# Twenty-four weight pieces narrowed in two groups instead of three, and a block's additions written ahead of its low parts

## The chip, the core and the metric

The kernel runs on one core of a Trainium2 chip. The core has five engines that work side by side, each through its own instructions in their written order: PE (TensorE, matrix products, with PEld for its weight loads), DVE (VectorE), ACT (ScalarE), POOL (GpSimd) and SP (SyncE, which here only issues DMAs). An engine that has to wait for another holds up everything behind it in its own order. PE accumulates in PSUM, which has few buffers; a buffer is free for the next product only when DVE or ACT has read it. The metric is device time of one execution in microseconds (us).

## What is computed

Three steps follow each other. An attention with decay (retention, 4 batches, 8 heads, 576 positions) gives x, 2304 tokens by 512. Then come two layers of two products each, 512 to 2048 to 512, with different functions between them:

```python
attn_out = _attn_ref(**attn_kwargs)
x = attn_out.transpose(0, 2, 1, 3).reshape(B * S, H * D)

def _moe_ref(x, w_in, w_out):          # layer 1
    h = x @ w_in
    g = np.maximum(0.01 * h, h)
    return (g @ w_out).astype(np.float32)

def _moe2_ref(x, w_in, w_out):         # layer 2
    h = x @ w_in
    g = h - np.tanh(h)
    return (g @ w_out).astype(np.float32)
```

The four weight matrices arrive as 64-bit floating-point numbers and have to be narrowed to 32 bits on the chip.

## The kernel before

**Products in three parts.** Each 32-bit operand is split into a high part and a low part, and a product is high times high, high times low and low times high. x lies in `xh` and `xl`, a weight piece in the two halves of `wp`.

**Groups, blocks, steps.** A layer's 2048 inner columns are 16 slices of 128, and four slices are a group, so each layer has four groups, which are called 0 to 3 here (the second and third group are groups 1 and 2). Within a group the 2304 tokens are cut into five blocks, called A, B, R, C and D in the order in which they run: A and B of 512 tokens, R (the rest) of 256, C and D of 512. A block has four steps, one for each slice `f`. Step s does `h_mm(s)` (12 matmuls into a PSUM tile `h`), ACT's function `act_a`, `chain`, and two steps later `o_mm` (12 matmuls into the block's PSUM tiles `a`). After a block's fourth step `evac` (line 273) adds the PSUM tiles to `acc` in four quarters d on DVE (line 291). In layer 1's last group, group 3, the sum is final, and each quarter is also split for layer 2: ACT copies it to `xh` (line 295) and DVE subtracts to get `xl` (line 296), quarter by quarter.

**PSUM.** The `a` tiles come from a ring of five buffers. A 512-token block takes four, and R takes two, since two of its quarters share one. So the last of C's four tiles needs the first of R's two back, for which R's first two quarters must have been added. Across the change of layer, the first block's second tile needs the first quarter of the block before, and so on.

**Weight pieces.** A layer's group has 8 pieces (4 slices, in and out), each 512 KB of 64-bit words. `load_piece` (line 109) brings one into one of two buffers `st`; `narrow_ops` (lines 112 to 159) narrows it on DVE in five instructions: `begin` (line 131), `clamp` (line 137), `shift` (line 142), `top` and `low` (both line 148). During each group of layer 1 the 8 pieces of the next group are narrowed. The pieces of layer 2's groups 1 to 3, 24 in all, are also narrowed during layer 1: as `spare` pieces, which `keep_piece` (line 163) writes to DRAM, and which `fetch_piece` (line 168) brings back during layer 2. `split_piece` (lines 174 and 175) makes the two halves on ACT and POOL.

**What sets the order.** `layers` (line 620) writes the order by hand. The narrowing instructions of a group are spread evenly, by number, over its steps (`plan`, line 649). In a step stand, in this order, `h_mm`, `chain`, `act_a`, `o_mm` of two steps before, up to four planned operations, `evac` of two steps before, and the other planned operations. So what is left of a step's narrowing stands ahead of a block's additions on DVE, and everything after them waits for the additions. The line that the change rewrites in the plan, and the span of the plan:

```python
spare = pieces_of(1, q[1]) if q[0] == 0 and q[1] else []
...
free = max(hi if spare else last + 1, lo + 9)
span = range(lo + 1, free)
```

So with a spare piece the plan of a group runs to its last step, and without one it ends three steps earlier.

Of the kernel before, what the change touches and what calls it, by code (L numbers as in the profile page):

```python
# [10 lines left out]
F32 = mybir.dt.float32  # L11
# [4 lines left out]
ALU = mybir.AluOpType  # L16
# [17 lines left out]
def retention_moe_moe(  # L34
# [16 lines left out]
    nc = tc.nc  # L51
# [9 lines left out]
    NG = NF // GF  # L61
# [6 lines left out]
    xh = keep.tile([P, KK, NT], F32R, name="xh")  # L68
    xl = keep.tile([P, KK, NT], F32R, name="xl")
# [35 lines left out]
    def load_piece(key):  # L105
        m, kind, f = key
        src = ((w1i, w1o), (w2i, w2o))[m][kind][f]
        st = stage.tile([P, 512], I64 if wide else F32, tag="st", name="st")
        nc.sync.dma_start(out=st, in_=src)
        raw[key] = st  # L110
# [55 lines left out]
    def fetch_piece(key):  # L166
        w = cw_pool[0].tile([P, 512], F32, tag="cw", name="cw")
        nc.sync.dma_start(out=w, in_=kept.pop(key))
        half[key] = w

    def split_piece(key):
        wf = half.pop(key)
        wp = wring.tile([P, 2, 512], F32R, tag=f"w{key[1]}", name="wp")
        nc.scalar.activation(out=wp[:, 0, :], in_=wf, func=AF.Copy)  # L174
        nc.gpsimd.tensor_tensor(  # L175
            out=wp[:, 1, :], in0=wf, in1=wp[:, 0, :].bitcast(F32), op=ALU.subtract
        )
        wt[key] = wp

    def pieces_of(m, g):  # L180
        return [(m, kind, g * GF + f) for f in range(GF) for kind in range(2)]
# [5 lines left out]
    def h_mm(s):  # L187
        m, g, t0, n, f = steps[s]
        w = wt[m, 0, g * GF + f]
        ps = pools["h"](s)  # L190
        for kk in range(KK):
            cs = slice(kk * P, (kk + 1) * P)
            for i, (wi, x) in enumerate(((0, xh), (0, xl), (1, xh))):
                nc.tensor.matmul(  # L194
                    out=ps[:, :n], lhsT=w[:, wi, cs], rhs=x[:, kk, t0:t0 + n],
                    start=kk == 0 and i == 0, stop=kk == KK - 1 and i == 2,
                )
        hp[s] = ps

    def act_a(s):  # L200
        m, g, t0, n, f = steps[s]
        W, tp = pools["w"], pools["t"]
        h = hp[s][:, :n]
        if m == 0:
            a = tp.tile([P, W], F32, tag="u", name="a")
            gt = pools["g"].tile([P, 2, W], F32R, tag="g", name="g")
            nc.scalar.activation(out=a[:, :n], in_=h, func=AF.Prelu, alpha=0.01)  # L207
            nc.scalar.activation(out=gt[:, 0, :n], in_=h, func=AF.Prelu, alpha=0.01)  # L208
            tmp[s] = a, gt
            return  # L210
        u = tp.tile([P, W], F32, tag="u", name="u")
        v = tp.tile([P, W], F32, tag="v", name="v")
        t_ = tp.tile([P, W], F32, tag="t", name="t")
        q = tp.tile([P, W], F32, tag="q", name="q")
        mk = tp.tile([P, W], F32, tag="mk", name="mk")
        nc.scalar.activation(out=u[:, :n], in_=h, func=AF.Square)  # L216
        nc.scalar.activation(out=t_[:, :n], in_=h, func=AF.Tanh)  # L217
        nc.gpsimd.tensor_tensor(out=v[:, :n], in0=t_[:, :n], in1=u[:, :n], op=ALU.mult)  # L218
        nc.scalar.activation(  # L219
            out=q[:, :n], in_=u[:, :n], func=AF.Square, scale=math.sqrt(RHO_C), bias=qb[:, 0:1]  # L220
        )
        nc.scalar.activation(out=mk[:, :n], in_=u[:, :n], func=AF.Relu, bias=qb[:, 1:2])  # L222
        tmp[s] = (v, t_, q, mk)
# [49 lines left out]
    def evac(s):  # L273
        m, g, t0, n, f = steps[s]
        if f != GF - 1:
            return
        width = n if m == 0 else DM
        cnt = KK if m == 0 else n // P
        pack = 512 // width
        ps = ac_ps.pop(s - f)  # L280
        for d in range(cnt):
            at = (d % pack) * width
            a = ps[d // pack][:, at:at + width]
            dst = acc_t[:, d, t0:t0 + n] if m == 0 else acc_n[:, t0 // P + d, :]
            if g == 0:
                if d % 2:
                    nc.scalar.activation(out=dst, in_=a, func=AF.Copy)
                else:
                    nc.vector.tensor_copy(out=dst, in_=a)
                continue  # L290
            nc.vector.tensor_tensor(out=dst, in0=a, in1=dst, op=ALU.add)  # L291
            if g < NG - 1:
                continue
            if m == 0:
                nc.scalar.activation(out=xh[:, d, t0:t0 + n], in_=dst, func=AF.Copy)  # L295
                nc.vector.tensor_tensor(  # L296
                    out=xl[:, d, t0:t0 + n], in0=dst,
                    in1=xh[:, d, t0:t0 + n].bitcast(F32), op=ALU.subtract,
                )
            else:  # L300
                nc.sync.dma_start(out=out[t0 + d * P:t0 + (d + 1) * P, :], in_=dst)

    def split_order(keys):

        return sorted(keys, key=lambda k: (k[2] + LAG * k[1], k[1]))

    def piece_ops(keys, split=True, spare=()):


        ops, late = [], []  # L310
        for j, key in enumerate(keys):
            part = narrow_ops(key)
            if j + 2 < len(keys):
                part.append(lambda k=keys[j + 2]: load_piece(k))
            ops += part[:3] + late + part[3:]
            late = [lambda k=key: split_piece(k)] if split else []
            if key in spare:
                late = [lambda k=key: keep_piece(k)]
        return ops + late
# [300 lines left out]
    def layers():  # L620
        with ExitStack() as mc:
            pools["t"] = mc.enter_context(tc.tile_pool(name="t1", bufs=2))
            pools["g"] = mc.enter_context(tc.tile_pool(name="g1", bufs=3))
            cw_pool[0] = mc.enter_context(tc.tile_pool(name="c1", bufs=2 * GF + 3))
            ps_h = mc.enter_context(tc.tile_pool(name="ps_h1", bufs=3, space=PSUM))
            pools["h"] = lambda s: ps_h.tile([P, 512], F32, tag="h", name="h")
            pools["a"] = mc.enter_context(tc.tile_pool(name="ps_a1", bufs=5, space=PSUM))
            pools["w"] = 512
            early[0] = False

            plan, splits = {}, {}
            groups = list(per_group)
            free = n_early
            for q, nxt in zip(groups, groups[1:]):
                lo, hi = per_group[q]
                lo, last = max(lo, free), hi - GF
                keys = split_order(pieces_of(*nxt))
                spare = pieces_of(1, q[1]) if q[0] == 0 and q[1] else []  # L640
                if q[0]:
                    ops = [lambda k=k: fetch_piece(k) for k in keys]
                else:
                    ops = piece_ops(keys + spare, split=False, spare=spare)
                    plan.setdefault(lo, []).extend([lambda k=k: load_piece(k) for k in keys[:2]])
                free = max(hi if spare else last + 1, lo + 9)
                span = range(lo + 1, free)
                for j, op in enumerate(ops):
                    plan.setdefault(span[j * len(span) // len(ops)], []).append(op)
                for key in keys:  # L650
                    at = last + key[2] % GF + (1 if key[1] == 0 else 1 + LAG)
                    splits.setdefault(at, []).append(key)
            end = len(steps)
            for s in range(n_early, end):
                h_mm(s)
                tight = s >= end - GF
                if tight:
                    act_a(s)
                if s > n_early:
                    chain(s - 1)  # L660
                if not tight:
                    act_a(s)
                if n_early <= s - LAG < end - GF:
                    o_mm(s - LAG)
                ops = plan.get(s, [])
                for op in ops[:4]:
                    op()
                if n_early <= s - LAG < end - GF:
                    evac(s - LAG)
                for op in ops[4:]:  # L670
                    op()
                for key in splits.get(s, ()):
                    split_piece(key)

            for s in range(end - GF, end):
                o_mm(s)
                if s == end - GF:
                    chain(end - 1)
                evac(s)
# [73 lines left out]
```

## Time and profile before

| | us |
|---|---|
| median of 3 runs | 907.11 |
| the runs | 906.95, 907.11, 910.55 |
| the profiled execution | 908.26 |
| its span, first to last instruction | 906.5 |
| PE busy | 870.4 (96%) |
| DVE busy | 550.9 (61%) |
| ACT busy | 378.1 (42%) |
| POOL busy | 422.9 (47%) |

Start with PE, which is busy for 96% of the span: only what makes PE stand still, or run at its lower clock, can be won without taking matmuls away. The profile's strip of 40 slices shows PE at seven tenths or less in the first three (retention), at nine or more almost everywhere else, and one dip in the middle and one at the end. The chain of waits that ended last goes through PE for 82% of the span. A shared engine such as DVE matters where PE waits for it, which is read place by place from the timeline.

### The profile page before, as it was taken

What the parts mean: (1) busy time and instruction counts of PE and PEld (TensorE: products, weight loads), DVE (VectorE), ACT (ScalarE), POOL (GpSimd) and SP (SyncE); (2) the same over time, 40 slices, a digit from 0 to 9 for tenths busy, and PEclk for the clock granted to TensorE, in tenths of its full rate; (3) what the DMA queues carried; (4) which work ended last, traced back from release to release, by engine and by line L of the source; (5) the groups of instructions that cost most, each with busy time, mean ns of one, the idle gap of its engine ahead of it and who ended that gap; (6) DMA issues with size and microseconds to landing.
All of it is one profiled execution on the core that took longest, in us unless ns stands there. A gap on an engine that the chain in (4) does not pass through costs nothing.

```text
span 906.5 us, 13256 instructions
## 1 busy us (share of the span) xinstructions
PE 870.4 (96%) x5024; PEld 745.0 (82%) x5024; DVE 550.9 (61%) x922; ACT 378.1 (42%) x767; POOL 422.9 (47%) x340
## 2 busy tenths in 40 slices
PE   6759999999999999999999899999999999999998
PEld 5659999988888889888878688888888888888886
DVE  6865434697894767666887744444555555555454
ACT  2333332242122222232323466676456655565553
POOL 4544342264233522252234564586446754585443
PEclk9989999999999999999999999999999999999999
DMA  8634332122262324322242300020000100001111
GB/s 288 221 117 137 124 106 100 70 95 92 93 196 66 110 93 128 105 94 70 93 134 86 129 13 0 1 66 28 1 1 24 35 1 1 1 1 47 47 47 70
DMA packets 28575, 70.96 MB, mean 78 GB/s; under 512 B 3296, under 2 KB 3680, under 8 KB 28512
## 3 DMA queue, kind: packets, MB, share of 16 engines
q1 hardware_dynamic: 27936, 69.74, 23.1%
q8 instruction: 39, 0.64, 0.3%
q10 hardware_dynamic: 576, 0.38, 0.1%
q14 instruction: 24, 0.20, 0.1%
HBM read 59.10 MB, written 11.01 MB: 77 GB/s over the span
## 4 chain that ended last, share of the span: by engine, by line
PE 82%; DVE 9%; ACT 3%; issue 2%; DMA 2%; POOL 1%; ACTq 0%; POOLq 0%; DVEq 0%
PE h L194 36%; PE a L266 35%; PE a L539 4%; PE x_b L514 3%; DVE cw L148 2%; DVE acc L291 1%; DVE xl L296 1%; ACT xh L295 1%; PE o L473 1%; DVE cw L137 1%; PE sc L397 1%; DVE cw L142 1%; PE o L461 1%; DVE st L444 1%; DMA st<-in_w2o 1%
## 5 line engine op out<-in xcount | busy, mean ns | idle before, releaser
L194 PE MATMUL h<-xh,wp 128*128 128x512 f32 (+1 forms) x1184 | 357.2, 368 | 0.0
L194 PEld LDWEIGHTS h<-xh,wp 128*128 128x128 f32 x1184 | 217.4, 190 | 37.6
L194 PE MATMUL h<-xl,wp 128*128 128x512 f32 (+1 forms) x592 | 217.9, 368 | 0.0
L266 PE MATMUL a<-wp,g 128*128 128x512 f32 x864 | 210.7, 391 | 4.2 <-DVE acc L291 1.9
L266 PEld LDWEIGHTS a<-wp,g 128*128 128x128 f32 x864 | 161.1, 188 | 38.9 <-DVE acc L291 2.8
L266 PE MATMUL a<-g,wp 128*128 128x512 f32 (+1 forms) x816 | 176.7, 365 | 3.2 <-DVE acc L291 2.2
L266 PEld LDWEIGHTS a<-g,wp 128*128 128x128 f32 x816 | 141.2, 189 | 28.8 <-DVE acc L291 2.6
L240 POOL TENSOR_TENSOR g<-v,g 128x512 fp32r<-128x512 f32 (+1 forms) x80 | 95.1, 1189 | 145.5 <-ACT g L239 145.4
L240 POOL TENSOR_TENSOR g<-a,g 128x512 fp32r<-128x512 f32 (+1 forms) x68 | 87.9, 1293 | 158.9 <-ACT g L208 138.7
L175 POOL TENSOR_TENSOR wp<-cw,wp 128x512 fp32r<-128x512 f32 x64 | 91.4, 1437 | 90.4 <-ACT wp L174 90.1
L194 PEld LDWEIGHTS h<-xl,wp 128*128 128x128 f32 x592 | 112.3, 190 | 18.8
L207 ACT ACTIVATE a<-h 128x512 f32<-128x512 f32 (+1 forms) x68 | 37.2, 548 | 210.0 <-PE h L194 207.2
L148 DVE SCALAR_TENSOR_TENSOR cw<-st,cw 128x512 uint32<-128x512 uint32 x128 | 117.0, 914 | 4.1
L291 DVE TENSOR_TENSOR acc<-a,acc 128x512 f32<-128x512 f32 (+1 forms) x114 | 74.4, 662 | 67.8 <-PE a L266 67.8
L233 DVE TENSOR_TENSOR h<-h,t 128x512 f32<-128x512 f32 (+1 forms) x80 | 51.5, 644 | 96.6 <-ACT t L217 96.6
L239 ACT ACTIVATE g<-v 128x512 fp32r<-128x512 f32 (+1 forms) x80 | 47.2, 589 | 148.5 <-DVE v L237 147.4
L218 POOL TENSOR_TENSOR v<-t,u 128x512 f32<-128x512 f32 (+1 forms) x80 | 95.1, 1189 | 12.8 <-ACT t L217 12.3
L234 DVE SCALAR_TENSOR_TENSOR v<-q,v 128x512 f32<-128x512 f32 (+1 forms) x80 | 56.6, 708 | 54.7 <-POOL v L218 53.7
L237 DVE COPY_PREDICATED v<-mk,h 128x512 f32<-128x512 uint32 (+1 forms) x80 | 54.9, 686 | 9.2 <-DVE v L234 1.4
L219 ACT ACTIVATE q<-u,qb 128x512 f32<-128x512 f32 (+1 forms) x80 | 54.5, 681 | 0.0
L222 ACT ACTIVATE mk<-u,qb 128x512 f32<-128x512 f32 (+1 forms) x80 | 54.3, 678 | 0.0
L216 ACT ACTIVATE u<-h 128x512 f32<-128x512 f32 (+1 forms) x80 | 43.6, 545 | 18.6 <-PE h L194 18.2
(60 smaller groups left out, 798.3 us busy)
## 6 DMA issues: line engine op xcount, KB each, us to landing
st<-in_w1i SPq DMA_DIRECT2D x16, 512.0 KB, 3.4
st<-in_w1o SPq DMA_DIRECT2D x16, 512.0 KB, 3.3
st<-in_w2i SPq DMA_DIRECT2D x16, 512.0 KB, 3.8
st<-in_w2o SPq DMA_DIRECT2D x16, 512.0 KB, 3.7
kept<-cw SPq DMA_DIRECT2D x24, 256.0 KB, 4.1
cw<-kept SPq DMA_DIRECT2D x24, 256.0 KB, 2.7
kv<-in_vn SPq DMA_DIRECT2D x16, 320.0 KB, 5.2
qk<-in_qT SPq DMA_DIRECT2D x16, 288.0 KB, 3.5
```

The costliest lines, as they stand in the source:

```text
L148: nc.vector.scalar_tensor_tensor(out=t["w"], in0=t[src], scalar=scalar, in1=t["w"], op0=op, op1=ALU.bitwise_or)
L175: nc.gpsimd.tensor_tensor(out=wp[:, 1, :], in0=wf, in1=wp[:, 0, :].bitcast(F32), op=ALU.subtract)
L194: nc.tensor.matmul(out=ps[:, :n], lhsT=w[:, wi, cs], rhs=x[:, kk, t0:t0 + n], start=kk == 0 and i == 0, stop=kk == KK - 1 and i == 2,)
L218: nc.gpsimd.tensor_tensor(out=v[:, :n], in0=t_[:, :n], in1=u[:, :n], op=ALU.mult)
L219: nc.scalar.activation(out=q[:, :n], in_=u[:, :n], func=AF.Square, scale=math.sqrt(RHO_C), bias=qb[:, 0:1])
L222: nc.scalar.activation(out=mk[:, :n], in_=u[:, :n], func=AF.Relu, bias=qb[:, 1:2])
L233: nc.vector.tensor_tensor(out=h, in0=h, in1=t_, op=ALU.subtract)
L234: nc.vector.scalar_tensor_tensor(out=v, in0=q, scalar=RHO_A, in1=v, op0=ALU.add, op1=ALU.mult)
L237: nc.vector.copy_predicated(out=v, mask=mk.bitcast(U32), data=h)
L240: nc.gpsimd.tensor_tensor(out=gt[:, 1, :n], in0=v, in1=gt[:, 0, :n].bitcast(F32), op=ALU.subtract)
L266: nc.tensor.matmul(out=o, lhsT=l, rhs=r, start=f == 0 and i == 0 and d % pack == 0, stop=f == GF - 1 and i == 2 and (d + 1) % pack == 0, s ...
L291: nc.vector.tensor_tensor(out=dst, in0=a, in1=dst, op=ALU.add)
```

## The change

Two places change. In the plan, the 24 spare pieces are no longer taken eight in each of groups 1, 2 and 3: the list of all 24 is cut in halves, twelve in group 1 and twelve in group 2, and group 3 narrows only the 8 pieces that layer 2's group 0 needs. In `evac`, in layer 1's group 3, the four additions and the four `xh` copies are written first, and the four subtractions for `xl` after them.

```diff
@@ evac
         ps = ac_ps.pop(s - f)
+        low_parts = []
         for d in range(cnt):
...
                 nc.scalar.activation(out=xh[:, d, t0:t0 + n], in_=dst, func=AF.Copy)
-                nc.vector.tensor_tensor(
-                    out=xl[:, d, t0:t0 + n], in0=dst,
-                    in1=xh[:, d, t0:t0 + n].bitcast(F32), op=ALU.subtract,
-                )
+                low_parts.append((d, dst))
             else:
                 nc.sync.dma_start(out=out[t0 + d * P:t0 + (d + 1) * P, :], in_=dst)
+
+        for d, dst in low_parts:
+            nc.vector.tensor_tensor(
+                out=xl[:, d, t0:t0 + n], in0=dst,
+                in1=xh[:, d, t0:t0 + n].bitcast(F32), op=ALU.subtract,
+            )
@@ layers
-                spare = pieces_of(1, q[1]) if q[0] == 0 and q[1] else []
+
+                kept_ones = [k for g in range(1, NG) for k in pieces_of(1, g)]
+                a, b = (len(kept_ones) * (q[1] - i) // (NG - 2) for i in (1, 0))
+                spare = kept_ones[max(a, 0):b] if q[0] == 0 and 0 < q[1] < NG - 1 else []
```

The order of PE, ACT and POOL is the same in both kernels; DVE and SP differ. Three places show how. In these rows `cw` is a piece being narrowed, `st` its raw words, `a` a PSUM tile, and a row with `x4` stands for four instructions.

On DVE in layer 1's group 1, the end of block B's stretch up to the four additions of block R (128x256). Before:

```order
L137 TENSOR_SCALAR cw<-cw 128x512
L142 TENSOR_SCALAR cw<-cw 128x512
L148 SCALAR_TENSOR_TENSOR cw<-st,cw 128x512 x2
L291 TENSOR_TENSOR acc<-a,acc 128x256 x4
L131 TENSOR_SCALAR cw<-st 128x512
```

Now:

```order
L137 TENSOR_SCALAR cw<-cw 128x512
L142 TENSOR_SCALAR cw<-cw 128x512
L148 SCALAR_TENSOR_TENSOR cw<-st,cw 128x512 x2
L131 TENSOR_SCALAR cw<-st 128x512
L137 TENSOR_SCALAR cw<-cw 128x512
L292 TENSOR_TENSOR acc<-a,acc 128x256 x4
L142 TENSOR_SCALAR cw<-cw 128x512
```

Between B's additions and R's stood 18 narrowing instructions and now stand 21; between A's and B's 19 and now 24. In group 2 the same two counts go from 18 to 22 and from 16 to 20.

On DVE in group 3, around block R's additions. Before:

```order
L148 SCALAR_TENSOR_TENSOR cw<-st,cw 128x512 x2
L131 TENSOR_SCALAR cw<-st 128x512
L291 TENSOR_TENSOR acc<-a,acc 128x256
L296 TENSOR_TENSOR xl<-acc,xh 128x256
L291 TENSOR_TENSOR acc<-a,acc 128x256
L296 TENSOR_TENSOR xl<-acc,xh 128x256
```

Now:

```order
L148 SCALAR_TENSOR_TENSOR cw<-st,cw 128x512 x2
L131 TENSOR_SCALAR cw<-st 128x512
L137 TENSOR_SCALAR cw<-cw 128x512
L292 TENSOR_TENSOR acc<-a,acc 128x256 x4
L302 TENSOR_TENSOR xl<-acc,xh 128x256 x4
L142 TENSOR_SCALAR cw<-cw 128x512
```

The additions are no longer interrupted by subtractions. Between B's additions and R's stood 16 narrowing instructions and now stand 10.

On DVE at the change from layer 1 to layer 2, where `h`, `v` and `mk` belong to layer 2's first two steps and the additions to layer 1's last block D. Before:

```order
L131 TENSOR_SCALAR cw<-st 128x512
L137 TENSOR_SCALAR cw<-cw 128x512
L142 TENSOR_SCALAR cw<-cw 128x512
L148 SCALAR_TENSOR_TENSOR cw<-st,cw 128x512 x2
L233 TENSOR_TENSOR h<-h,t 128x512
L234 SCALAR_TENSOR_TENSOR v<-q,v 128x512
L237 COPY_PREDICATED v<-mk,h 128x512
L291 TENSOR_TENSOR acc<-a,acc 128x512
L296 TENSOR_TENSOR xl<-acc,xh 128x512
L291 TENSOR_TENSOR acc<-a,acc 128x512
```

Now:

```order
L292 TENSOR_TENSOR acc<-a,acc 128x512 x4
L302 TENSOR_TENSOR xl<-acc,xh 128x512 x4
L233 TENSOR_TENSOR h<-h,t 128x512
L234 SCALAR_TENSOR_TENSOR v<-q,v 128x512
L237 COPY_PREDICATED v<-mk,h 128x512
L292 TENSOR_TENSOR acc<-a,acc 128x512 x4
L302 TENSOR_TENSOR xl<-acc,xh 128x512 x4
L233 TENSOR_TENSOR h<-h,t 128x512
```

Here the first additions and subtractions are block C's. The two narrowed pieces that stood ahead of layer 2's first step are gone, and D's four additions stand together.

## Rows read from the trace of the kernel before

**Rows 1.** Windows, groups 1, 2, 3: us; PE, PEld, DVE, ACT, POOL busy (instructions); clock; DMA.

```profile
205.45:304.79 99.34, 99.34 (x485) 84.13 (x484) 71.36 (x105) 25.33 (x50) 38.00 (x30) 1.00 0.32 106
304.79:403.45 98.66, 98.66 (x482) 83.58 (x481) 66.79 (x102) 24.19 (x48) 35.54 (x29) 1.00 0.33 107
403.45:507.20 103.75, 100.60 (x480) 84.07 (x479) 80.84 (x112) 32.51 (x63) 37.86 (x27) 0.98 0.29 94
```

**Rows 2.** Timeline, PE, marks one group apart: start, us, instruction, count.

```profile
342.23 2.91 PE L266 MATMUL a<-g,wp 128*128 128x512 f32 x12
...
405.36 2.88 PE L266 MATMUL a<-g,wp 128*128 128x512 f32 x12
...
440.89 2.91 PE L266 MATMUL a<-g,wp 128*128 128x512 f32 x12
...
509.66 1.52 PE L266 MATMUL a<-wp,g 128*128 128x512 f32 x6
...
551.99 2.91 PE L266 MATMUL a<-wp,g 128*128 128x512 f32 x12
```

**Rows 3.** Timeline, PE in group 3, with idle time and who ended it.

```profile
453.09 1.58 PE L266 MATMUL a<-g,wp 128*128 128x256 f32 x11 [0.68 <-POOL g L240]
...
465.80 1.15 PE L266 MATMUL a<-g,wp 128*128 128x512 f32 x3 [2.16 <-DVE acc L291]
466.75 0.63 PE L194 MATMUL h<-xh,wp 128*128 128x512 f32 x1
...
473.69 0.39 PE L194 MATMUL h<-xh,wp 128*128 128x512 f32 x1
...
493.43 2.79 PE L266 MATMUL a<-g,wp 128*128 128x512 f32 x11 [0.32 <-POOL g L240]
```

**Rows 4.** Timeline, DVE in group 3, block R's first two additions.

```profile
464.08 0.42 DVE L291 TENSOR_TENSOR acc<-a,acc 128x256 f32<-128x256 f32 x1
464.98 0.43 DVE L296 TENSOR_TENSOR xl<-acc,xh 128x256 fp32r<-128x256 f32 x1 [0.48 <-ACT xh L295]
465.32 0.42 DVE L291 TENSOR_TENSOR acc<-a,acc 128x256 f32<-128x256 f32 x1
```

**Rows 5.** Timeline, PE at the change of layer.

```profile
512.07 0.96 PE L266 MATMUL a<-wp,g 128*128 128x512 f32 x3 [0.89 <-DVE acc L291]
514.06 1.56 PE L266 MATMUL a<-wp,g 128*128 128x512 f32 x3 [1.03 <-DVE acc L291]
515.42 0.63 PE L194 MATMUL h<-xh,wp 128*128 128x512 f32 x1
...
520.56 0.51 PE L266 MATMUL a<-wp,g 128*128 128x512 f32 x1 [1.18 <-ACT g L239]
521.98 2.80 PE L266 MATMUL a<-wp,g 128*128 128x512 f32 x11 [0.92 <-POOL g L240]
```

**Rows 6.** Timeline, DVE at the change of layer.

```profile
504.69 0.68 DVE L233 TENSOR_TENSOR h<-h,t 128x512 f32<-128x512 f32 x1
...
510.72 0.69 DVE L296 TENSOR_TENSOR xl<-acc,xh 128x512 fp32r<-128x512 f32 x1 [2.84 <-ACT xh L295]
```

**Rows 7.** Timeline, DVE in groups 1 and 2 (last row): narrowing and additions.

```profile
227.89 1.41 DVE L148 SCALAR_TENSOR_TENSOR cw<-st,cw 128x512 uint32<-128x512 uint32 x2
...
230.59 2.52 DVE L148 SCALAR_TENSOR_TENSOR cw<-st,cw 128x512 uint32<-128x512 uint32 x2
...
244.47 2.74 DVE L291 TENSOR_TENSOR acc<-a,acc 128x512 f32<-128x512 f32 x4 [3.00 <-PE a L266]
247.13 0.42 DVE L142 TENSOR_SCALAR cw<-cw 128x512 uint32<-128x512 uint32 x1
...
259.93 1.46 DVE L291 TENSOR_TENSOR acc<-a,acc 128x256 f32<-128x256 f32 x4
...
358.57 1.48 DVE L291 TENSOR_TENSOR acc<-a,acc 128x256 f32<-128x256 f32 x4 [1.43 <-PE a L266]
```

**Rows 8.** Timeline, PE in group 1, block C's first `o_mm`.

```profile
263.18 2.88 PE L266 MATMUL a<-g,wp 128*128 128x512 f32 x12
```

## The prediction

> **What bounds the kernel now.** I read the strip of PE first, then PE's busy time by group, then the timelines of PE and DVE at the places where PE stood. In groups 1 and 2 of layer 1 PE is busy for the whole of both windows, 99.34 of 99.34 us and 98.66 of 98.66 us [rows 1]. So nothing done to DVE, ACT or POOL can make these two groups shorter. The window of group 3 and the change of layer is different: PE is busy for 100.60 of 103.75 us and its mean granted clock is 0.98 [rows 1]. The loss there is measured best by a mark that returns once a group. From group 2's mark to the same mark in group 3 it is 440.89 - 342.23 = 98.66 us; from there to the same mark in layer 2 it is 551.99 - 440.89 = 111.10 us [rows 2]. The matmuls between the marks are the same, so about 111.10 - 98.66 = 12.44 us are lost in the second stretch. It divides by another mark, a group's first `o_mm`: in the undisturbed stretch it comes 405.36 - 342.23 = 63.13 us after the first mark, and in the disturbed one 509.66 - 440.89 = 68.77 us [rows 2]. So 5.64 us are lost within group 3 and 6.80 us at the change of layer.
>
> The waits of PE say why. In group 3 PE waits 2.16 us for an addition of DVE and 0.68 and 0.32 us for POOL [rows 3]. After the long wait its matmuls take 0.63 us, as they do at 515.42 [rows 3, 5], where one takes 0.39 a little later [rows 3]: in such a stretch the granted clock is at its lower level, 1.2 GHz instead of 2.4. At the change of layer PE waits 0.89 and 1.03 us for DVE's additions, then 1.18 us for ACT and 0.92 us for POOL [rows 5]. The seven waits make 7.18 us; the other 5.3 us are the two stretches at 1.2 GHz, so at most 2.6 us each, and the ends of the matmuls before each wait, which the rows count as busy.
>
> **Part 1, eight spare pieces leave group 3.** They are 40 narrowing instructions on DVE and 8 writes to DRAM and 8 loads on SP. DVE's total does not change, only its place. What PE waited for at 465.80 is the release of the PSUM buffer that holds R's first two quarters. DVE came to the first of these additions at 464.08, and its row shows no wait for PE [rows 4]: R's products were there, and DVE was late, because 16 narrowing instructions stood between B's additions and R's. Now 10 do, six fewer at about 0.71 us (the price is in part 3), so DVE is there some 4 us earlier from this alone. B's additions are earlier too, for the same reason. The two waits for POOL have the same root: ACT stands at its `xh` copies, which need DVE's additions, and POOL's next low part waits for ACT behind them. At the change of layer two pieces stood ahead of layer 2's first step on DVE, so that its `h` subtraction began only at 504.69 [rows 6]. Those pieces are gone, and nothing but D's products holds D's additions.
>
> **Part 2, additions ahead of the low parts.** Before, the second addition waited for the first subtraction, and that for ACT: from 464.08 to 465.32 is 1.24 us for each of R's quarters [rows 4]. Four additions in a row take 1.46 us, or 0.37 each [rows 7]. So R's buffer comes back 0.9 us earlier by this. At D it counts for more. DVE waited 2.84 us for ACT between D's first and second addition [rows 6], because ACT had the first step's four functions of layer 2 in front of its copy. Four additions in a row take 2.74 us [rows 7] and now wait for nobody but PE. What is late next is the second step of layer 2: its first subtraction on DVE still stands behind D's four low parts, and these behind ACT. Four low parts at 0.69 us [rows 6] are 2.8 us. What this can still cost lies between nothing and the 1.18 and 0.92 us that PE waits there for ACT and POOL today [rows 5], 2.1 us. I take 0.4, near nothing, because D's additions no longer alternate with the low parts, so that all of them end several us earlier against PE than they do now.
>
> **Part 3, four pieces more in groups 1 and 2.** This is the part that can cost. PE shows no wait in these groups today, so the price has to be bounded by DVE's slack. In group 1 DVE had 19 narrowing instructions between A's additions and B's. They began at 227.89, and DVE was ready 3.00 us before 244.47, at 241.47 [rows 7]: 13.58 us, or 0.715 each with the waits for loads in it. From 247.13 to 259.93 it had 18 in 12.80 us, 0.711 each [rows 7]. Now there are 24 and 21. The first stretch then ends at 227.89 + 24 x 0.715 = 245.05, 0.6 us after PE is ready; the additions end at 247.7; the second stretch ends at 247.7 + 21 x 0.711 = 262.6. R's first two quarters are back 0.8 us later, at 263.4. PE needs that buffer for the last quarter of C's first `o_mm`, at 263.18 [rows 8] plus three quarters of 2.72, that is at 265.2. The margin shrinks from 4.5 to 1.8 us and holds. In group 2 DVE waited 1.43 us for R's products [rows 7], and four instructions more are 2.8 us, so it comes 1.4 us late with the same 4.5 us allowed. Blocks C and D of both groups have more slack still. I take no wait for this part.
>
> The bound on the other side: a piece not held up by POOL takes about 2.80 us (three instructions like the 0.42 us one with their gaps, and a pair at 1.41); a pair met by POOL takes 2.52 us instead of 1.41 [rows 7]. If each piece is met once and waits 0.3 us for its load, an instruction costs (2.80 + 1.11 + 0.3) / 5 = 0.84 us. Then the stretches end at 248.1 and, after additions to 250.7, at 268.4, and PE waits some 4 us, with up to 2.6 us for a stretch at 1.2 GHz behind it. I take the middle of the trace, 0.71, since it was measured in the same places with the same work of POOL beside it.
>
> **SP.** It loses 8 pieces in group 3 and gets 4 more in each of the others. The order of a load and of the write of the piece before it stays as it was, so a piece's load still has one piece's time to land. What is queued behind them, layer 2's 24 reads of kept pieces, starts earlier, beside PE.
>
> **Sum.** 12.44 us come back, less 0.4 us for the second step of layer 2 and 0.2 for short waits that DVE's fuller order may bring: 11.8 us. Against the profiled execution that is 908.26 - 11.8 = 896.5 us. That execution stood 1.15 us above the median, so for the median 907.11 - 11.8 = 895.3 us.
>
> **Rivals.**
> 1. *R is late in group 1.* The margin of 1.8 us is used up when an instruction costs above 0.75 us in both stretches. The wait is then 1 to 4 us, with the clock up to 6.6. Time: 896 to 902, say 899.5.
> 2. *The change of layer is not cured.* D's low parts and the second step hold PE as before, and only group 3's 5.64 us come back: 901.5. For it speaks that two of the four waits there were for ACT and POOL [rows 5]; against it, that both had waited for DVE, which had just been held by D.
> 3. *The edit does not reach the waits.* Some other chain holds PE in group 3 as late as DVE did, and the time stays between 903 and 907. Against it speaks that the releaser of the longest wait is named and ends 0.06 us before PE goes on [rows 3, 4].
> 4. *DVE becomes the bound of groups 1 and 2, slower.* In group 1 20 pieces at 2.80 us and the additions, 4 x 2.74 + 1.46 = 12.4 us [rows 7], make 68.4 us. POOL is busy 38.00 us there and 35.54 in group 2 [rows 1]. If POOL held DVE up for all of that time, the groups would need 106.4 and 103.9 us against 99.34 and 98.66, 12.3 us more in sum, and 5.2 with a stretch at 1.2 GHz in each: 17.5 less 11.8 saved is 5.7 us, 912.8. The saving is spent when the share f of POOL's time that falls on DVE makes 2 x 68.4 + 73.54 f = 198.0 + 6.6, that is f = 0.92. In the trace DVE is busy 71.36 us in group 1 [rows 1]; less some 13 of additions and copies that is 58 us for about 84 instructions, where 2.80 a piece would make 47. So 11 of the 38 us fell on DVE.
>
> The Trainium skill's page "SBUF — State Buffer", section "Who interferes with whom", says that DVE and GpSimd share a pair of ports by an exclusive lock: the one that comes second waits for the whole of the other's instruction. That rule speaks against the change and would be rival 4. The lengthened pair in [rows 7] agrees with it for a single instruction; the group's total does not bear out the full price, since much of POOL's time fell where DVE was waiting or adding.
>
> **How the numbers follow.** Forecast 0.72, rival 1 0.12, rival 2 0.07, rival 3 0.05, rival 4 0.04. The range goes from 893.8, where all 12.44 us come back and the run is 0.9 us better still, to 900.5, which takes in most of rival 1 and leaves out the others. About 0.5%, 4.5 us, is what a measurement of this kernel can tell from no change. Faster than 902.6 are the forecast, rival 1 and most of rival 2: 0.89. Within it falls the rest of rival 2 and rival 3: 0.07. Slower: 0.04.
>
> **What would show it.** Right: the same marks stand 98 to 99.5 us apart from group 2 to layer 2; PE has no wait for an addition in group 3 and none of 1 us at the change of layer; the clock is 1.00 in that window; the `xl` subtractions come four in a row. R's additions in group 1 begin near 262.6, and PE's busy time still fills groups 1 and 2. Wrong: a wait of PE for DVE at C's first `o_mm` in group 1, followed by matmuls of 0.63 us (rival 1); waits for ACT or POOL at layer 2's second step (rival 2); additions that begin later from block to block (rival 4).

## The result, and the profile after

The changed kernel takes 895.25 us (median of 6 runs, 894.57 to 896.93) against 907.64 us before (6 runs, 906.26 to 910.55). The ratio is 0.986, with a 95% interval from 0.9842 to 0.9878. The forecast was 895.3 us; the profiled execution takes 895.5 us with a span of 893.7.

The windows of the three groups of layer 1 (us; busy time of PE, PEld, DVE, ACT and POOL; clock; DMA share; GB/s), which answer to [rows 1]:

```profile
205.45:304.79 99.34, 99.34 (x485) 84.15 (x484) 83.70 (x125) 25.18 (x50) 40.18 (x30) 1.00 0.43 138
304.79:403.45 98.66, 98.66 (x482) 83.59 (x481) 78.30 (x120) 24.16 (x48) 36.51 (x29) 1.00 0.44 139
403.45:497.00 93.55, 93.55 (x459) 79.38 (x458) 46.77 (x72) 32.85 (x63) 32.24 (x26) 1.00 0.16 54
```

The third window ends earlier than before and holds 21 matmuls fewer, so the lengths of the two are not compared. PE now fills all three windows and its clock is 1.00 in the third. DVE's busy time rose by 12.3 us in group 1 and by 11.5 in group 2, and PE did not notice. The marks of PE, which answer to [rows 2]:

```profile
342.05 2.91 PE L266 MATMUL a<-g,wp 128*128 128x512 f32 x12
...
440.71 2.91 PE L266 MATMUL a<-g,wp 128*128 128x512 f32 x12
...
503.84 2.88 PE L266 MATMUL a<-wp,g 128*128 128x512 f32 x12
...
539.67 2.91 PE L266 MATMUL a<-wp,g 128*128 128x512 f32 x12
```

From group 2 to group 3 they stand 98.66 us apart, as before; from group 3 to layer 2, 539.67 - 440.71 = 98.96 us instead of 111.10. So 12.14 us came back, which is the whole difference of the two times but a few tenths. The first `o_mm` of layer 2 stands 503.84 - 440.71 = 63.13 us after the mark, as in an undisturbed group: group 3 lost nothing any more. The other 0.30 us are lost at the change of layer.

On DVE, blocks B and R in group 3, where [rows 4] stood:

```profile
441.61 2.74 DVE L292 TENSOR_TENSOR acc<-a,acc 128x512 f32<-128x512 f32 x4 [8.15 <-PE a L266]
444.26 3.03 DVE L302 TENSOR_TENSOR xl<-acc,xh 128x512 fp32r<-128x512 f32 x4
...
457.05 1.47 DVE L292 TENSOR_TENSOR acc<-a,acc 128x256 f32<-128x256 f32 x4 [3.59 <-PE a L266]
```

DVE now waits for PE before both, 8.15 and 3.59 us: it was late at R before and is early now. At the change of layer, where [rows 6] stood:

```profile
494.36 0.70 DVE L233 TENSOR_TENSOR h<-h,t 128x512 f32<-128x512 f32 x1 [10.60 <-ACT t L217]
...
499.28 2.73 DVE L292 TENSOR_TENSOR acc<-a,acc 128x512 f32<-128x512 f32 x4 [2.00 <-PE a L266]
501.93 3.59 DVE L302 TENSOR_TENSOR xl<-acc,xh 128x512 fp32r<-128x512 f32 x4
```

Layer 2's first step has DVE waiting 10.60 us for it, where it used to wait for DVE, and before D's additions DVE waits 2.00 us for PE. Group 1, on DVE and then on PE, against [rows 7, 8]:

```profile
244.29 2.74 DVE L292 TENSOR_TENSOR acc<-a,acc 128x512 f32<-128x512 f32 x4
...
261.88 1.40 DVE L292 TENSOR_TENSOR acc<-a,acc 128x256 f32<-128x256 f32 x4
```

```profile
263.00 2.88 PE L266 MATMUL a<-g,wp 128*128 128x512 f32 x12
```

DVE comes to B's additions without a wait, so it is just in time, and to R's at 261.88. R's first two quarters are back by about 262.6, and PE needs the buffer at 263.00 + 2.04 = 265.0. The margin is 2.4 us.

### The profile page after: what moved, and what is told of

It reads as the page before. It is cut to its first block, busy times and chain, and to the rows that moved or that the text cites. A ratio compares the mean times of both kernels' runs of the same rounds, so it can differ in the third digit from the quotient of the medians.

```text
span 893.7 us, 13252 instructions
## 1 busy us (share of the span) xinstructions
PE 868.6 (97%) x5024; PEld 747.0 (84%) x5024; DVE 541.6 (61%) x922; ACT 378.0 (42%) x767; POOL 421.2 (47%) x340
## 4 chain that ended last, share of the span: by engine, by line
PE 92%; DMA 2%; DVE 2%; POOL 1%; ACT 1%; issue 1%; SPq 0%; POOLq 0%; ACTq 0%
PE h L194 40%; PE a L266 40%; PE a L543 4%; PE x_b L518 3%; DMA kv<-in_vn 2%; PE sc L401 1%; PE o L477 1%; PE o L465 1%; POOL wp L175 1%; PE x_c L434 1%; PE x_a L407 0%; POOL kv L378 0%; DVE cw L148 0%; DVE cw L142 0%; PE x_c L477 0%
## 5 line engine op out<-in xcount | busy, mean ns | idle before, releaser
L148 DVE SCALAR_TENSOR_TENSOR cw<-st,cw 128x512 uint32<-128x512 uint32 x128 | 113.3, 885 | 4.0
L131 DVE TENSOR_SCALAR cw<-st 128x512 uint32<-128x512 uint32 x56 | 40.5, 724 | 18.6 <-DMA st<-in_w2i 6.4
```

The source lines that it names most:

```text
L148: nc.vector.scalar_tensor_tensor(out=t["w"], in0=t[src], scalar=scalar, in1=t["w"], op0=op, op1=ALU.bitwise_or)
```

## The experiments

### Each part alone

The first kernel (e1) has the new plan and the old order in `evac`, the second (e2) the old plan and the new order.

```diff
 e1, against the changed kernel
-                low_parts.append((d, dst))
+                nc.vector.tensor_tensor(
+                    out=xl[:, d, t0:t0 + n], in0=dst,
+                    in1=xh[:, d, t0:t0 + n].bitcast(F32), op=ALU.subtract,
+                )

 e2, against the changed kernel
-                spare = kept_ones[max(a, 0):b] if q[0] == 0 and 0 < q[1] < NG - 1 else []
+                spare = pieces_of(1, q[1]) if q[0] == 0 and q[1] else []
```

> Only the plan is changed (twelve spare pieces in groups 1 and 2, none in group 3); additions and low parts alternate as before. Theory (what cost time in group 3 was DVE coming late behind its narrowing): all 5.6 us within group 3 come back; at the change of layer D's additions no longer wait for narrowing, but each still waits for ACT's copy behind the first step's four functions, so the low parts end about 2.5 us later than in the changed kernel and PE waits 1 to 3 us at layer 2's second step. Time 896.5 to 900, say 898. Rival (the alternation itself is what holds the additions): the waits at the change of layer stay, 6.8 us of loss, time about 901.5.

The plan alone takes 900.43 us (4 runs, 898.66 to 900.66), ratio to before 0.9911 (0.9886 to 0.9936). In group 3 PE shows no wait. DVE, from B's last subtraction to R's first addition, and the one row of PE that is longer than its like:

```profile
448.74 0.69 DVE L296 TENSOR_TENSOR xl<-acc,xh 128x512 fp32r<-128x512 f32 x1 [0.70 <-ACT xh L295]
...
456.82 0.42 DVE L291 TENSOR_TENSOR acc<-a,acc 128x256 f32<-128x256 f32 x1 [0.19 <-PE a L266]
```

```profile
487.29 3.31 PE L266 MATMUL a<-g,wp 128*128 128x512 f32 x12
```

DVE is ready for R at 456.63, 7.2 us after B's last subtraction; in the kernel before it took 12.0 us (452.12 to 464.08). PE's row of 3.31 us instead of 2.88 stands where PE waited 0.32 us for POOL before [rows 3], so 0.43 us are still lost there. At the change of layer, PE and then DVE:

```profile
511.59 0.49 PE L266 MATMUL a<-wp,g 128*128 128x512 f32 x1 [1.94 <-ACT g L239]
513.00 4.36 PE L266 MATMUL a<-wp,g 128*128 128x512 f32 x11 [0.92 <-POOL g L240]
```

```profile
499.48 0.69 DVE L291 TENSOR_TENSOR acc<-a,acc 128x512 f32<-128x512 f32 x1 [1.99 <-PE a L266]
501.72 0.69 DVE L296 TENSOR_TENSOR xl<-acc,xh 128x512 fp32r<-128x512 f32 x1 [1.55 <-ACT xh L295]
```

The waits are where the theory put them and of the size it gave (2.86 us), and a stretch at the lower clock follows: 11 matmuls take 4.36 us where 2.8 is usual, at a mean granted clock of 0.60. With that the time comes out just above the expected span.

> Only the order in the last group's evac is changed; eight spare pieces stay in each of groups 1, 2 and 3. Theory of the prediction (both parts carry, the plan the larger one within group 3): R's additions come about 0.9 us earlier by their own order and a few us by B's, which may just lift the wait at C; narrowing still stands ahead of layer 2's first step. Time about 903, with a wait of DVE's additions left. Rival (either part alone gives DVE the few us that it is late): B's additions and low parts take 5.4 us instead of 8, so DVE reaches R near 461.5 instead of 464.1, no wait at C, and at the change of layer only 0 to 1 us is left. Time about 896.

The order alone takes 896.03 us (4 runs, 895.44 to 896.29), ratio 0.9866 (0.9842 to 0.9889). The theory that I had carried over from the prediction fell here, and the rival stood. PE's marks, then DVE at B and R:

```profile
441.09 2.91 PE L266 MATMUL a<-g,wp 128*128 128x512 f32 x12
...
540.01 2.91 PE L266 MATMUL a<-wp,g 128*128 128x512 f32 x12
```

```profile
441.98 2.74 DVE L292 TENSOR_TENSOR acc<-a,acc 128x512 f32<-128x512 f32 x4 [0.94 <-PE a L266]
444.64 3.03 DVE L302 TENSOR_TENSOR xl<-acc,xh 128x512 fp32r<-128x512 f32 x4
...
458.02 1.41 DVE L292 TENSOR_TENSOR acc<-a,acc 128x256 f32<-128x256 f32 x4
```

The marks stand 98.92 us apart, as with both parts. With all sixteen pieces still in group 3, DVE comes to R at 458.02 instead of 464.08 [rows 4], earlier than the rival's 461.5. To see why, here are B's first addition and last subtraction in the kernel before:

```profile
444.07 0.68 DVE L291 TENSOR_TENSOR acc<-a,acc 128x512 f32<-128x512 f32 x1
...
451.43 0.69 DVE L296 TENSOR_TENSOR xl<-acc,xh 128x512 fp32r<-128x512 f32 x1 [0.70 <-ACT xh L295]
```

Alternating, B's eight instructions took 451.43 + 0.69 - 444.07 = 8.05 us; in two runs of four they take 444.64 + 3.03 - 441.98 = 5.69. So B gives DVE 2.4 us back. A's eight instructions, read in the same way, took 8.41 us (422.56 to 430.97) and take 5.13 (422.76 to 427.89), so A gives 3.3 back, and B could start 2.1 us earlier. The rest of the way to R is shorter as well: the sixteen narrowing instructions between B and R take 10.4 us instead of 12.0, with fewer of them lengthened and shorter waits for loads.

### Which block's order matters

With the old plan, the additions are put first in some blocks only: in A and B (f1), in R (f2), in D (f3).

```diff
-                low_parts.append((d, dst))
+                if t0 < 1024:            # f1; f2: t0 == 2048; f3: t0 == 1536
+                    low_parts.append((d, dst))
+                else:
+                    nc.vector.tensor_tensor(
+                        out=xl[:, d, t0:t0 + n], in0=dst,
+                        in1=xh[:, d, t0:t0 + n].bitcast(F32), op=ALU.subtract,
+                    )
```

> The plan of before (eight spare pieces in groups 1, 2 and 3); additions ahead of the low parts only in blocks A and B of group 3, in R, C and D alternating as before. Theory (in group 3 the alternation makes DVE some 2.5 us later at each 512-token block, and R only shows what A and B left): DVE reaches R near 459, PE does not wait at C's first o_mm, the 5.6 us of group 3 come back and the 6.8 us at the change of layer stay: 901 to 904, say 902. Rival (R's own alternation holds its buffer): the wait of 2.2 us at C stays, about 907.

> The plan of before; additions ahead of the low parts only in block R. Theory (R only shows what A and B left): DVE still reaches R at 464, two additions take 0.8 instead of 1.7 us, so the wait at C shrinks from 2.2 to about 1.3 us and the rest stays: 905 to 908, say 906.5. Rival (R's own alternation holds its buffer): no wait at C, about 902.

> The plan of before; additions ahead of the low parts only in block D. Theory: group 3's 5.6 us stay; at the change of layer D's additions come at 507 to 510 without a wait for ACT, so PE's two waits for additions go, and up to 1.5 us are left at layer 2's second step: 901 to 904, say 902. Rival (the two narrowed pieces ahead of layer 2's first step hold it): waits of 3 us and more stay there, 905 or above.

Before took 909.62 us beside these runs (8 runs, 905.63 to 910.81), a wide spread, so I go by the marks and the waits as much as by the times. A and B: 903.68 us, ratio 0.9946 (0.9916 to 0.9977). R: 905.83 us, 0.9959 (0.9944 to 0.9973). D: 903.90 us, 0.9941 (0.9917 to 0.9964). In f1, DVE's first addition of R, then PE's marks, with its longest wait and the row behind it:

```profile
457.16 0.41 DVE L292 TENSOR_TENSOR acc<-a,acc 128x256 f32<-128x256 f32 x1
```

```profile
438.75 2.91 PE L266 MATMUL a<-g,wp 128*128 128x512 f32 x12
...
502.52 1.52 PE L266 MATMUL a<-wp,g 128*128 128x512 f32 x6
...
513.41 0.50 PE L266 MATMUL a<-wp,g 128*128 128x512 f32 x1 [2.80 <-ACT g L239]
514.84 4.38 PE L266 MATMUL a<-wp,g 128*128 128x512 f32 x11 [0.92 <-POOL g L240]
...
546.46 2.91 PE L266 MATMUL a<-wp,g 128*128 128x512 f32 x12
```

In f2, the same marks of PE, and PE at C and at the change of layer:

```profile
439.79 2.91 PE L266 MATMUL a<-g,wp 128*128 128x512 f32 x12
...
463.79 0.98 PE L266 MATMUL a<-g,wp 128*128 128x512 f32 x3 [1.28 <-DVE acc L292]
...
506.06 1.52 PE L266 MATMUL a<-wp,g 128*128 128x512 f32 x6
...
516.96 0.78 PE L266 MATMUL a<-wp,g 128*128 128x512 f32 x1 [2.79 <-ACT g L239]
518.38 5.06 PE L266 MATMUL a<-wp,g 128*128 128x512 f32 x11 [0.64 <-POOL g L240]
...
550.93 2.91 PE L266 MATMUL a<-wp,g 128*128 128x512 f32 x12
```

In f3, PE at C and at the change of layer, and DVE at D's additions:

```profile
466.61 0.96 PE L266 MATMUL a<-g,wp 128*128 128x512 f32 x3 [2.57 <-DVE acc L292]
...
517.22 0.50 PE L266 MATMUL a<-wp,g 128*128 128x512 f32 x1 [1.15 <-ACT g L239]
```

```profile
508.03 2.47 DVE L292 TENSOR_TENSOR acc<-a,acc 128x512 f32<-128x512 f32 x4
```

A and B put first let DVE come to R 18.4 us after PE's mark (457.16 - 438.75) instead of 23.2 (464.08 - 440.89), and PE has no wait at C, although R itself still alternates. R put first only shortens that wait, from 2.16 [rows 3] to 1.28 us, as expected. So what the alternation adds to the wait at C comes mostly from A and B, and R itself adds 0.9 us. The narrowing ahead of R adds to it too, since e1 has no such wait while all blocks alternate. D put first takes PE's two waits for additions at the change of layer away and leaves the waits for ACT and POOL.

What I had not expected is what became of the time won early. In f1 and f2 the wait for ACT at layer 2's second step grew from 1.18 us [rows 5] to 2.80 and 2.79. The longer wait itself costs nothing: PE goes on 10.9 us after layer 2's first `o_mm` in all three kernels (520.56 - 509.66, 513.41 - 502.52, 516.96 - 506.06), and DVE and ACT come to this place as much earlier as PE does (7.1 us in f1, 3.6 in f2). What differs is where the stretch at 1.2 GHz lies. In the kernel before it lies in front of the wait for ACT (clock 0.57 from 514 to 518 us), so it only fills time in which PE would have waited. In f1 and f2 the matmuls in front of this wait run at full speed, and the stretch follows behind it, where nothing hides it: eleven matmuls take 4.38 and 5.06 us instead of 2.80 [rows 5]. Why the clock fell at one wait and not at the other is not shown.

By the marks f1 gets 5.0 of group 3's 5.6 us back (the first `o_mm` of layer 2 comes 63.77 us after the mark instead of 68.77) and loses 1.6 us more at the change of layer (43.94 us from there to the last mark instead of 42.33): 3.4 are left. f2 gets 2.5 back and loses 2.5 more, so nothing is left (111.14 us). In f2 the measured ratio says 2.7 to 5.6 parts in a thousand faster and its one profiled execution, the slowest of its five, says no gain; which of the two is typical I leave open. The profiled execution of f3 is the slowest of its four as well (906.52 us): by its marks only 2.3 us come back.

### Where the pieces stand

With the additions first everywhere, the plan is moved: 16 and 8 spare pieces in groups 1 and 2 (e3), all 24 in group 1 (e4), none in group 1 and 12 in groups 2 and 3 (f4).

```diff
-                a, b = (len(kept_ones) * (q[1] - i) // (NG - 2) for i in (1, 0))
-                spare = kept_ones[max(a, 0):b] if q[0] == 0 and 0 < q[1] < NG - 1 else []
+                cuts = [0, 0, 16, 24, 24]   # e3; e4: 24, 24, 24; f4: 0, 12, 24
+                spare = kept_ones[cuts[q[1]]:cuts[q[1] + 1]] if q[0] == 0 else []
```

> The changed kernel, but with 16 spare pieces in group 1 and 8 in group 2. Between A's additions and B's in group 1 stand 28 narrowing instructions, between B's and R's 25. Theory (0.70 us each, waits for loads in it): DVE reaches B's additions near 250, PE waits some 2 us in R's first o_mm, and 2 to 3.6 us in C's first, with one or two stretches at 1.2 GHz. Time 898 to 906, say 902. Rival (POOL's time falls on DVE in full): 24 pieces at 2.80, 12.4 of additions and 40 of POOL are 119.6 us for a group of 99.3, so about 915. If neither, and 895, then the slack of groups 1 and 2 is larger than I worked out.

It takes 904.34 us (10 runs, 900.5 to 911.19), ratio 0.9965 (0.9937 to 0.9994). Its profiled execution takes 900.54. In it PE waits once in the whole of layer 1, at C's first `o_mm` in group 1; PE, DVE, and group 1's window:

```profile
267.30 1.65 PE L266 MATMUL a<-g,wp 128*128 128x512 f32 x3 [3.40 <-DVE acc L292]
```

```profile
266.50 1.41 DVE L292 TENSOR_TENSOR acc<-a,acc 128x256 f32<-128x256 f32 x4
```

```profile
205.45:304.79 99.34, 95.94 (x457) 80.76 (x456) 85.00 (x133) 22.59 (x45) 37.11 (x27) 0.97 0.54 160
```

So block R is where the margin ends first, as the prediction's first rival had it, at four pieces more than the change puts there; the wait in R's own first `o_mm` that I also expected did not come, since DVE reached B's additions at 245.74 and not near 250. The runs spread over 10.7 us, where the changed kernel's spread over 2.4; the profile shows only one of them, the second fastest.

> The changed kernel, but with all 24 spare pieces in group 1. 163 narrowing instructions stand between group 0's last additions and group 1's last. Theory (0.70 to 0.72 us each, 12.4 us of additions): 127 us of DVE for 99.3 of PE, less some 5 us of slack at the ends, with stretches at 1.2 GHz of 1.7 us at several waits: 20 to 30 us more than the changed kernel, 913 to 928, say 920. Rival (POOL's time falls on DVE in full): 32 x 2.80 + 12.4 + 40 = 142 us, about 938.

It takes 934.66 us (4 runs, 933.78 to 937.14), ratio 1.0296 (1.0268 to 1.0325): slower than the theory's range of 913 to 928, and under the rival's 938. The stretch in which group 1 runs, as a window, and DVE's narrowing in it by lines (busy us, mean ns, idle us before):

```profile
205.00:344.00 139.00, 110.88 (x500) 92.15 (x498) 117.79 (x181) 27.11 (x54) 44.79 (x32) 0.91 0.56 169
```

```profile
L148 DVE SCALAR_TENSOR_TENSOR cw<-st,cw 128x512 uint32<-128x512 uint32 x64 | 52.5, 820 | 2.1
L142 DVE TENSOR_SCALAR cw<-cw 128x512 uint32<-128x512 uint32 x33 | 19.4, 589 | 1.1
L131 DVE TENSOR_SCALAR cw<-st 128x512 uint32<-128x512 uint32 x33 | 19.0, 575 | 16.6 <-DMA st<-in_w2i 8.3 <-DMA st<-in_w1i 4.5 <-DMA st<-in_w2o 3.1
L137 DVE TENSOR_SCALAR cw<-cw 128x512 f32<-128x512 f32 x33 | 18.9, 573 | 1.1
```

Here DVE is the bound: it is busy for 117.79 us and waits 16.6 for loads. PE stands for 139.00 - 110.88 = 28.1 us, and at a mean clock of 0.91 it spends about 2 x 0.09 x 139 = 25 us at 1.2 GHz, which costs half of that, 12.5; the sum of 40.6 answers to the 38.7 us between the two profiled executions. My price missed in two places. An instruction cost (109.8 busy + 16.6 of waits for loads + 4.3 of short gaps) / 163 = 0.80 us instead of 0.70 to 0.72, since with no other slack a wait for a load shows at about every second piece. And the lower clock cost 12.5 us in all, where one such stretch costs about 1.6 (in f3, below). POOL's share, the rival's matter, is 109.8 less some 89 us that 33 pieces take undisturbed (three instructions at 0.43 and a pair at 1.42), so by this estimate about 20 of POOL's 44.8 us fell on DVE. That they are POOL's is seen row by row: each of the 26 narrowing rows that are over 0.15 us longer than undisturbed lies beside an instruction of POOL. The rival's full price is not borne out even with DVE at its limit.

> The order of the changed kernel (all additions first), but no spare piece in group 1 and twelve in each of groups 2 and 3. Between A's and B's additions in group 3 stand 22 narrowing instructions and four low parts, between B's and R's 20 and four. Theory (0.70 us each, 5.5 us for a block's additions and low parts): DVE reaches R near 462.8, PE waits 1 to 3 us at C with a stretch at 1.2 GHz behind it, and 0 to 2 us at the change of layer: 897 to 904, say 899.5. Rival (with the additions first it does not matter in which group the pieces are narrowed): 895 to 896.5.

It takes 901.47 us (4 runs, 901.33 to 902.08), ratio 0.991 (0.9893 to 0.9926). PE at C in group 3 and at layer 2's second step:

```profile
464.00 0.96 PE L266 MATMUL a<-g,wp 128*128 128x512 f32 x3 [1.61 <-DVE acc L292]
...
513.76 0.50 PE L266 MATMUL a<-wp,g 128*128 128x512 f32 x1 [1.43 <-ACT g L239]
```

DVE reaches R at 463.20, near the 462.8 expected. By the marks 1.9 us are lost in group 3 and 4.0 at the change of layer (PE's marks at 440.59 and 545.15, layer 2's first `o_mm` at 505.62), where I had expected at most 2. The place of the pieces does matter: with 12 in group 3 the wait at C is back even with the additions first. With 8 there (e2) it is not, and with none (the changed kernel) not either.

## Why the prediction was right

**The loss and its size.** Right. The loss of 12.44 us was read from marks of PE, and 12.14 came back. That the gain has this ceiling, since PE is busy in groups 1 and 2, is what made the time come out within 0.1 us; most of that nearness is luck, since the runs of one kernel differ by 2 us. The bound of 2.6 us for a stretch at 1.2 GHz was wide: in f3 one costs 1.6. The stretch at the change of layer cost next to nothing, as f1 and f2 show, because it lay in front of a wait that it only shortened; the prediction counts both as if each were paid.

**Part 1, the pieces that leave group 3.** Right in mechanism for the longest wait, and near in size: with the plan alone DVE takes 4.8 us less from B to R, where I had put some 4, and PE has no wait for an addition in group 3. The two waits for POOL, which I put down to the same root, do not both go with the pieces: at the second PE still loses 0.43 us with the plan alone, and nothing with the order alone (layer 2's first `o_mm` at 504.22, 63.13 us after the mark), so it goes with the order.

**Part 2, the order of additions and low parts.** The mechanism was right and the size was not. I priced it at R alone, 0.9 us, and did not add up that the same order had made A 3.3 and B 2.4 us longer ahead of R. In truth the order alone brings all that both parts bring: its marks stand 98.92 us apart and theirs 98.96, and the two medians, 896.03 and 895.25 us, differ by less than the runs of one kernel do. At the change of layer it is the part that counts: the plan alone leaves 2.86 us of waits and a stretch at the lower clock there. The step of the prediction that says "six fewer, so DVE is there some 4 us earlier" is true, but it was not needed. The sum did not show this, because both parts end at the same ceiling.

**Part 3, four pieces more in groups 1 and 2.** Right. I put R's additions at 262.6 with a margin of 1.8 us; they began at 261.88, with 2.4. The kernel with four pieces more in group 1 broke at this place. The change sits some four pieces from its own limit there.

**What is late next.** I kept 0.4 us for layer 2's second step and 0.2 for short waits; 0.30 are lost, at that step.

**The rivals.** None came. The second, that the change of layer is not cured, is near to what the plan alone does (900.43 us against 901.5). The fourth, DVE as the bound, takes twelve spare pieces more in group 1 than the change puts there; then it is 26 us slower than before, partly by POOL, partly by loads and partly by the clock. The page of the Trainium skill "SBUF — State Buffer" ("Who interferes with whom") says the second comer waits for the whole of the other's instruction. The traces agree for single instructions (a pair of 2.52 us instead of 1.41 [rows 7], beside an instruction of POOL of 1.28), and in e4, where DVE has no slack, about 20 of POOL's 44.8 us come to DVE as waiting.

## What to carry to other kernels

When two engines alternate on a chain of pieces, write all of one engine's pieces first if its result frees something another engine waits for; the price of the alternation is paid in every block that has it, so add it over the blocks that come before the wait, and not only at the wait. When a change has two parts with one ceiling, ask what each does alone before it is called needed. Time won early can be lost again later, so follow the marks up to the next place at which PE waits: in f1 and f2 the stretch at the lower clock moved from in front of a wait, where it was hidden, to behind it, where it was paid.

## What the runs showed that I had not expected

Not every short wait of PE is followed by a stretch at its lower clock. After the wait of 2.16 us in the kernel before, and of 2.57 in f3, matmuls of 0.63 us follow; after 1.61 us in f4 and 1.28 in f2 none do at that place. Group 3 in f4 and in f3:

```profile
440.00:480.00 40.00, 38.39 (x206) 32.99 (x205) 34.94 (x59) 12.11 (x26) 9.79 (x8) 1.00 0.57 162
```

```profile
440.00:480.00 40.00, 36.94 (x194) 31.44 (x194) 31.87 (x53) 11.26 (x24) 10.18 (x8) 0.96 0.41 123
```

In f3 a mean clock of 0.96 over 40 us means some 2 x 0.04 x 40 = 3.2 us at 1.2 GHz, which costs 1.6 us on top of the wait; in f4 little is paid beyond the wait itself (1.9 us by the marks). The length of the wait alone does not decide it: at the change of layer waits of 1.15 and 0.91 us in f3 are followed by eleven matmuls in 4.37 us, and waits of 1.43 and 0.92 us in f4 by eleven in 2.76. What does decide it is not shown. Also, the runs spread over 10.7 us with sixteen pieces in group 1 (ten runs) and over 2.4 us with twelve (six runs); with all 24 there it is 3.4 us (four runs), and the cause of the spread stays open.
